# Tile 0 of the second LayerNorm transposed in four matmuls and evicted by ScalarE in three pieces, with all five engine queues in a new order

## The chip, the cores and the metric

The kernel runs on one core of one Trainium2 chip. The metric is device time in microseconds, from launch to the last output byte; lower is better. A core has five instruction queues that run side by side and wait for each other by semaphores: TensorE (PE, matmuls; its weight loads are shown as PEld), VectorE (DVE), ScalarE (ACT), GpSimd (POOL) and SyncE (SP, which here issues nearly all DMAs). Within a queue, instructions run in the order in which they stand.

## The reference

Two pre-LayerNorm blocks on a bfloat16 input of 2048 rows by 448 columns: linear attention with 16 heads of 28, then a gated MLP of width 1792.

```python
def _A_ref(x, wqkv, wo):                       # D = 448, H = 16, Dh = 28
    q, k, v = split_heads(x @ wqkv)
    phi = lambda t: jnp.where(t > 0, t + 1, jnp.exp(t)) + 1e-6
    pq, pk = phi(q), phi(k)
    kv = jnp.einsum("bhsd,bhse->bhde", pk, v)
    z = jnp.einsum("bhsd->bhd", pk)
    num = jnp.einsum("bhqd,bhde->bhqe", pq, kv)
    den = jnp.einsum("bhqd,bhd->bhq", pq, z)[..., None] + 1e-6
    return merge_heads(num / den) @ wo

def _B_ref(x, w_gate, w_up, w_down):           # width 1792
    return (gelu_tanh(x @ w_gate) * (x @ w_up)) @ w_down

h = x + _A_ref(layernorm(x), A_wqkv, A_wo)
out = h + _B_ref(layernorm(h), B_w_gate, B_w_up, B_w_down)
```

`B_x` is not used.

## The kernel before

The 2048 rows are 16 tiles of 128. The whole kernel is a list of named tasks (one queue each, one or a few instructions), built by `G.add`/`op`, which records what each reads and writes. Five strings in `ORDERS` then say, by task number, in which order each queue runs its tasks (PE, ACT, DVE, POOL, SP), and semaphore waits are derived from the recorded reads and writes. `HOLD` only picks which of several waits comes last on an instruction. A task marked `mw=True` may place a wait in front of its k-th matmul (`W(k)`) rather than its first.

Names used below (t is the tile, line numbers are those of the kernel before):

- First LayerNorm. `bnst1_t`, `bnag1_t` (DVE, L486, L487) give mean and variance, `ln1_t` and `rstd1_t` (ACT, L493, L495) the reciprocal deviation. Tiles 0 to 3: `normD_t` (DVE, L508) normalizes, `tr0_t` and `tr1_t` (PE, L516) transpose two 128-column chunks each into PSUM, `evxA_t` (ACT, L521) and `evxD_t` (DVE, L523) copy them to `xnT`. Tiles 4 to 15: `negm1_t` and `normP_t` (POOL, L490, L526) normalize, and `xT_t` (SP, L528) is a DMA transpose.
- Projections. `k_t` and `q_t` (PE, L542), four matmuls each, into one of four PSUM banks taken in turn. `ek_t`, `ck_t`, `pk_t` (ACT L553, DVE L554 and L555) make phi(k); `eq_t` and `rq_t` (ACT, L569, L570) are the exponential and the Relu of q. The first two matmuls of `k_t` read what `evxA_t` wrote, the last two what `evxD_t` wrote.
- `pt4_t`, or `pt3_t` and `pt1_t` (PE, L561), accumulate the normalized input against phi(k) over all 16 tiles. From the sums follow `z1`, `z0` (the denominator), `kv`, `kvm`, `w2_c` and their evictions `evpD_3`, `evpA_c`, `evwA_c`, `evwD_c`.
- Attention output in pairs of tiles p. Tiles 0 and 1: `t1d_0`/`t1p_1`, `dr`, `rd`, `pn` (the denominator; L598 to L604), `tro_0`, `tro_1` (PE transposes), `evo_0`, `evo_1` (ACT, L629), `out1_t` (PE, L692). Later pairs use `drP`, `rdP`, `pnP` (DVE, L614 to L617), the DMA transpose `oT_p` and `outA_p`, `outB_p` (PE, L702, L703).
- Second LayerNorm. `hr_t` (DVE, L708) adds the residual, `bnst2`, `bnag2`, `ln2`, `rstd2` as above. Tiles 0 and 1: `nhD_t` (DVE, L720) normalizes to `hn`, `wr64_t` (DVE, L722) appends a copy of columns 0 to 63 at column 448, `trh_t` (PE, L729) transposes seven 128-column chunks into PSUM, and `evhA_0` (ACT, L733) or `evhD_1` (DVE, L735) copies all seven to `hnT`. Later tiles go through POOL and the DMA transpose `hT_t`.
- Gated MLP. `gu2_v` and `gu4_v` (PE, L806 and L808) compute gate and up products side by side: the gate matmuls read partitions 0 to 63 of a chunk of `hnT`, the up matmuls partitions 64 to 127. This is why `hnT` has seven chunks for 448 columns: chunks 0 to 3 hold the columns in one arrangement, chunks 4 to 6 hold them shifted by 64, so that every 64 columns are found once in the upper and once in the lower half. `geW`, `ge0`, `ge1` (ACT, L826) are the gelu, `hm` (DVE, L828) the product, `downA_p`, `downB_p` (PE, L772) the last matmuls, `fo` and `do` the residual and the output DMA.
- `tbl2` (ACT, L837) loads the activation table of gelu. In the kernel before it stands behind everything in the list `exps`: all exponentials, all `rq_t` and `evhA_0`.

Of the kernel before, what the change touches and what calls it, by code (L numbers as in the profile page):

```python
# [8 lines left out]
AF = mybir.ActivationFunctionType  # L9
# [114 lines left out]
}  # L124


# [173 lines left out]
def bass_sequential_preLN__linear_attn_block__glu_gated_geglu__prompt_kernel(  # L300
    nc, A_x, A_wqkv, A_wo, B_x, B_w_gate, B_w_up, B_w_down, out
):
    S, D, FF, H, DH = 2048, 448, 1792, 16, 28
# [594 lines left out]
```

## Time and profile before

| | |
|---|---|
| median of 3 runs | 189.8 us (189.75 to 190.27) |
| the profiled execution | 189.66 us, of which the span of its instructions is 187.7 us |
| PE busy | 183.3 us, 98% of the span, 1822 matmuls |
| DVE, ACT, POOL busy | 129.1 us, 73.7 us, 52.6 us |

The remaining 1.96 us of the profiled execution lie outside the span. A row of the timeline view gives start, duration, engine, line, operation, tile written and tiles read, form, and in square brackets idle time ahead of it with what ended it; equal neighbours are merged and counted. A matmul row's duration includes the drain of the last one, so neighbouring rows overlap. The windows view gives the busy time of each engine in a stretch, the waits view the idle time of an engine by what ended it.

### The profile page before, as it was taken

To read this page: it belongs to the slowest core of one execution; us is meant where nothing else is said; L and a number is where in the kernel's file an instruction comes from. 1 tells how busy PE (TensorE), PEld (TensorE's weight loads), DVE (VectorE), ACT (ScalarE), POOL (GpSimd) and SP (SyncE) were. 2 spreads that over 40 slices of the span, in tenths; PEclk is the share of its full clock that TensorE was granted. 3 is DMA by queue.
4 is the path that set the end of the run, shared out by engine and by line. 5 is a ranking of instruction groups with operands and counts; after the bars stand their busy time and mean duration, and the time that the engine had idled before them with its cause. 6 is when DMAs were issued, how large, how long until landed. Compare 5 with 4: busy or idle time off the path is not lost.

```text
span 187.7 us, 4436 instructions
## 1 busy us (share of the span) xinstructions
PE 183.3 (98%) x1822; PEld 123.4 (66%) x1822; DVE 129.1 (69%) x315; ACT 73.7 (39%) x197; POOL 52.6 (28%) x91
## 2 busy tenths in 40 slices
PE   7799999999999999999999999999999999999995
PEld 7445555645699899977777777777755555454553
DVE  4999897999997999898858546362745244335432
ACT  3878752799933122324132241222242222224100
POOL 6077920524638196412460000007300000000000
PEclk9999999999999999999999999999999999999999
DMA  5994558999398316900222800000093000002024
GB/s 165 379 245 89 100 100 187 219 218 186 63 240 179 75 35 119 147 5 0 48 52 42 154 3 0 0 3 0 9 147 93 3 2 24 3 0 98 3 73 147
DMA packets 35076, 17.17 MB, mean 91 GB/s; under 512 B 26736, under 2 KB 33648, under 8 KB 35056
## 3 DMA queue, kind: packets, MB, share of 16 engines
q1 hardware_dynamic: 34432, 16.37, 40.9%
q10 hardware_dynamic: 624, 0.52, 0.8%
q8 instruction: 14, 0.23, 0.6%
q14 instruction: 6, 0.05, 0.1%
HBM read 8.26 MB, written 1.84 MB: 54 GB/s over the span
## 4 chain that ended last, share of the span: by engine, by line
PE 96%; DVE 2%; DMA 1%; issue 0%
PE ps L808 24%; PE ps L806 22%; PE ps L772 19%; PE ps L542 13%; PE ps L561 6%; PE ps L702 3%; PE ps L753 3%; PE ps L703 2%; DMA x_sb<-in_A_x_dram 1%; DVE st L486 1%; PE ps L692 1%; PE ps L729 1%; PE ps L668 0%; PE ps L516 0%; PE ps L651 0%; DVE xnn L508 0%
## 5 line engine op out<-in xcount | busy, mean ns | idle before, releaser
L808 PE MATMUL ps<-hnT,wgu_sb 64*128 64x512 bf16 (+1 forms) x490 | 88.7, 333 | 0.0
L806 PE MATMUL ps<-hnT,wgu_sb 64*128 64x512 bf16 (+1 forms) x490 | 88.5, 333 | 0.0
L826 ACT ACTIVATE gl<-ps 128x256 bf16<-128x256 f32 (+1 forms) x98 | 35.7, 415 | 88.1 <-PE ps L806 88.0
L828 DVE TENSOR_TENSOR hh<-ps,gl 128x256 bf16<-128x256 f32 (+1 forms) x98 | 41.0, 454 | 41.4 <-ACT gl L826 41.0
L808 PEld LDWEIGHTS ps<-hnT,wgu_sb 64*128 64x128 bf16 x490 | 45.4, 94 | 13.1 <-DVE hh L828 1.5
L806 PEld LDWEIGHTS ps<-hnT,wgu_sb 64*128 64x128 bf16 x490 | 45.6, 94 | 11.1 <-DVE hnT L735 0.3
L772 PE MATMUL ps<-wd_sb,hh 64*128 64x448 bf16 x392 | 40.6, 349 | 0.0
L772 PEld LDWEIGHTS ps<-wd_sb,hh 64*128 64x128 bf16 x392 | 26.6, 94 | 11.0
L542 PE MATMUL ps<-wqk_sb,xnT 128*128 128x448 bf16 x128 | 27.4, 353 | 0.0
L486 DVE BATCH_NORM_STATS2 st<-x_sb 128x6 f32<-128x448 bf16 x32 | 19.2, 610 | 1.6 <-DMA x_sb<-in_A_x_dram 1.6
L542 PEld LDWEIGHTS ps<-wqk_sb,xnT 128*128 128x128 bf16 x128 | 12.0, 98 | 11.4 <-DVE pk L555 0.7
L613 POOL TENSOR_TENSOR t<-pq,zbc 128x448 f32<-128x448 bf16 x12 | 13.1, 1113 | 17.7 <-DVE pq L611 10.7
L561 PE MATMUL ps<-pk,xnn 128*128 128x448 bf16 x64 | 13.9, 352 | 0.0
L498 POOL TENSOR_SCALAR ln<-mv 128x2 f32<-128x2 f32 x7 | 2.0, 287 | 41.3 <-DVE mv L487 41.1
L702 PE MATMUL ps<-w,pqnT 64*128 64x448 bf16 x49 | 11.5, 349 | 0.1
L703 PE MATMUL ps<-pt_sb,pqnT 64*128 64x448 bf16 x49 | 11.5, 349 | 0.0
L553 ACT ACTIVATE e<-ps 128x448 bf16<-128x448 f32 x16 | 8.6, 539 | 5.1 <-PE ps L542 5.0
L708 DVE TENSOR_TENSOR x_sb<-ps,x_sb 128x448 bf16<-128x448 f32 x16 | 9.5, 614 | 1.2 <-PE ps L703 1.2
L737 POOL TENSOR_SCALAR hn<-x_sb,nm,rs 128x448 bf16<-128x448 bf16 x14 | 10.1, 733 | 0.5
L561 PEld LDWEIGHTS ps<-pk,xnn 128*128 128x128 bf16 x64 | 6.3, 98 | 5.8 <-DVE pk L555 0.4
L555 DVE SCALAR_TENSOR_TENSOR pk<-ps,e 128x448 bf16<-128x448 f32 x16 | 9.8, 617 | 0.2
L526 POOL TENSOR_SCALAR xnn<-x_sb,nm,rs 128x448 bf16<-128x448 bf16 x12 | 9.0, 750 | 2.3 <-ACT rs L495 2.0
(80 smaller groups left out, 155.2 us busy)
## 6 DMA issues: line engine op xcount, KB each, us to landing
out_dram<-x_sb SPq DMA_DIRECT2D x15, 112.0 KB, 1.8
wd_sb<-in_B_w_down_dram SPq DMA_DIRECT2D x1, 1568.0 KB, 9.4
x_sb<-in_A_x_dram SPq DMA_DIRECT2D x3, 448.0 KB, 6.0
wgu_sb<-in_B_w_gate_dram SPq DMA_DIRECT2D x1, 896.0 KB, 11.9
wgu_sb<-in_B_w_up_dram SPq DMA_DIRECT2D x1, 896.0 KB, 16.7
wgu_sb<-in_B_w_gate_dram SPq DMA_DIRECT2D x1, 672.0 KB, 5.9
wgu_sb<-in_B_w_up_dram SPq DMA_DIRECT2D x1, 672.0 KB, 8.4
wo_sb<-in_A_wo_dram SPq DMA_DIRECT2D x1, 392.0 KB, 7.7
```

Of the source, the lines that this page charges most:

```text
L486: op("dve", lambda e: e.bn_stats(st[:, t, :], src_ap), [b_src], [b_st[t]], "bnst%s_%d" % (tag, t))
L542: ins = e.matmul(ps[:, bk, 0:D], xnT[:, t, k, :], wqk_sb[:, k, c0:c0 + D], start=(k == 0), stop=(k == 3))
L561: ins = e.matmul(ps[:, BK_PT[c], 0:D], xnn[:, t % XN_R, c * 128:(c + 1) * 128], pk[:, ip, :], start=(t == 0), stop=(t == T - 1))
L613: op("pool", lambda e, n=n: e.tensor_tensor(t1[:, n, :, 0:DH], pq[:, a + n, :].rearrange("p (h d) -> p h d", h=H), zbc[:, :].rearrange("p ...
L702: e.matmul(ps[:, BK_OUT[0], 0:D], pqnT[ra, i2, sg // 2, :], w2[ra, sg // 2, :], start=(sg == 0), stop=(sg == 5))
L703: ins = e.matmul(ps[:, BK_OUT[1], 0:D], pqnT[rb, i2, 3 + (sg + 1) // 2, :], w2s[rb, sg // 2, :], start=(sg == 0), stop=(sg == 5))
L737: op("pool", lambda e, t=t, sh=sh: e.tensor_scalar(hn[:, sh, 0:D], x_sb[:, t, :], nm2[:, t:t + 1], rs2[:, t:t + 1], ALU.add, ALU.mult), [b ...
L772: ins = e.matmul(ps[:, bko[half][n], 0:D], hh[rows, j, sl[n]], wd_sb[rows, j, :], start=(j == 0 and (half == 0 or p == 6)), stop=(j == NJ ...
L806: first = e.matmul(psG[:, jj * N:(jj + 1) * N], wgu_sb[A_, k, j * 128:(j + 1) * 128], hnT[A_, ka_, c0:c0 + N], start=(k == 0), stop=(k == ...
L808: ins = e.matmul(psU[:, jj * N:(jj + 1) * N], wgu_sb[B_, k, j * 128:(j + 1) * 128], hnT[B_, kb_, c0:c0 + N], start=(k == 0), stop=(k == NK ...
L826: G.add("act", lambda e, gi=gi, cs_=cs_, psG=psG: e.activation(gl[:, gi, cs_], psG[:, cs_], AF.Gelu_apprx_tanh), r=[b_ps[BK_G[i]]], w=b_gl ...
L828: op("dve", lambda e, dst=dst, srcU=srcU, srcL=srcL: e.tensor_tensor(dst, srcU, srcL, ALU.mult), [b_ps[BK_U[i]]] + b_glh, [b_ar[j_][t % HR ...
```

## The change

1. `trh_0` makes four transposes (chunks 0 to 3) instead of seven. `evhA_0`, one ACT instruction over seven chunks, becomes three: `evhF_0` copies chunks 0 to 3 as they are, `evhS_0` and `evhT_0` make chunks 4 to 6 by writing the upper 64 partitions of one chunk to the lower half and the other way round. `gu2_0` waits for all three.
2. `trh_0` and `trh_1` wait for `wr64` only ahead of the one transpose that needs it.
3. The list ahead of `tbl2` holds only exponentials: `rq_t` and the evictions of tile 0 are out of it.
4. `ORDERS` and `HOLD` are new for all five queues.

```diff
@@ q_tile
-            act_exp(lambda e: e.activation(pq[:, t, :], ps[:, bk, 0:D], AF.Relu), [b_ps[bk]], [b_pq[t]], "rq_%d" % t)
+            op("act", lambda e: e.activation(pq[:, t, :], ps[:, bk, 0:D], AF.Relu), [b_ps[bk]], [b_pq[t]], "rq_%d" % t, after=[tbl1])
@@ a2_pair
-                    def ftrh(e, sh=sh, tvh=tvh):
+                    def ftrh(e, W, t=t, sh=sh, tvh=tvh):
                         ins = None
-                        for k in (0, 1, 2, 4, 5, 6, 3):
+                        for m, k in enumerate((0, 1, 2, 3) if t == 0 else (0, 1, 2, 4, 5, 6, 3)):
+                            W(m)
                             ko = k * 128 if k < 4 else (k - 4) * 128 + 64
                             ins = e.transpose(tvh[:, k, :], hn[:, sh, ko:ko + 128], ident[:])
                         return ins
-                    G.add("pe", ftrh, r=[b_hn[sh], b_hnd[sh], b_ident], w=[b_ps[BK_TH[t]]], name="trh_%d" % t)
+                    G.add("pe", ftrh, r=[(b_hn[sh], 0), (b_hnd[sh], 6 if t else 3), (b_ident, 0)], w=[(b_ps[BK_TH[t]], 0)], name="trh_%d" % t, mw=True)
                     if t == 0:
-                        exps.append(op("act", lambda e, hr8=hr8, tvh=tvh: e.activation(hnT[:, :, hr8], tvh, AF.Identity), [b_ps[BK_TH[t]]], [b_hnT[t]], "evhA_%d" % t))
+                        op("act", lambda e, hr8=hr8, tvh=tvh: e.activation(hnT[:, 0:4, hr8], tvh[:, 0:4, :], AF.Identity), [b_ps[BK_TH[t]]], [b_hnT[t]], "evhF_%d" % t)
+                        op("act", lambda e, hr8=hr8, tvh=tvh: e.activation(hnT[A_, 4:7, hr8], tvh[B_, 0:3, :], AF.Identity), [b_ps[BK_TH[t]]], [b_hnS[0]], "evhS_%d" % t)
+                        op("act", lambda e, hr8=hr8, tvh=tvh: e.activation(hnT[B_, 4:7, hr8], tvh[A_, 1:4, :], AF.Identity), [b_ps[BK_TH[t]]], [b_hnS[1]], "evhT_%d" % t)
@@ gu_chunk
-                G.add("pe", fngu, r=[b_hnT[t % HR] for t in tiles] + [b_wg[j0 * 128 >= FC], (b_wu[j0 * 128 >= FC], 1)], ...
+                G.add("pe", fngu, r=[b_hnT[t % HR] for t in tiles] + (b_hnS if t0 == 0 else []) + [b_wg[j0 * 128 >= FC], (b_wu[j0 * 128 >= FC], 1)], ...
@@ ORDERS, first string (PE)
-    "30 36 38 45 47 67 54 56 72 77 63 65 80 85 71 90 76 84 105 100 89 115 120 130 104 154 119 142 134 178 166 146"
+    "30 38 36 47 45 67 56 72 54 65 63 77 80 85 71 90 76 84 105 120 100 89 115 142 104 130 119 166 191 154 134 178"
```

What the new order does is seen at three places.

PE, from `pt4_1` on, after the first four K tiles. Rows of `ps<-wqk_sb,xnT` are projections, four matmuls each; rows of `ps<-pk,xnn` are `pt4`. Before:

```order
L561 MATMUL ps<-pk,xnn 128x448 x8
L542 MATMUL ps<-wqk_sb,xnT 128x448 x8
L561 MATMUL ps<-pk,xnn 128x448 x4
L542 MATMUL ps<-wqk_sb,xnT 128x448 x12
L561 MATMUL ps<-pk,xnn 128x448 x4
```

The same place now:

```order
L562 MATMUL ps<-pk,xnn 128x448 x8
L543 MATMUL ps<-wqk_sb,xnT 128x448 x12
L562 MATMUL ps<-pk,xnn 128x448 x4
L543 MATMUL ps<-wqk_sb,xnT 128x448 x8
L562 MATMUL ps<-pk,xnn 128x448 x4
```

The row of x8 before is `q_2 k_4`, that of x12 is `k_5 q_3 k_6`; now they are `q_2 q_3 k_4` and `k_5 k_7`. Further on the K tiles run 4, 5, 7, 6, 9, 11, 8, 10, 13, 12, 14, 15 (before: 4, 5, 6, 8, 7, 10, 9, 11, 12, 13, 14, 15), and the DMA transposes `xT_t` on SP are issued as 4, 5, 7, 6, 9, 11, 8, 10, 13, 14, 12, 15 (before: 4, 5, 6, 8, 7, 10, 9, 11, 12, 13, 14, 15).

DVE, from the eviction `evxD_2` (the first COPY) on. BN_STATS are `bnst1` of tiles 4 and 5, `e1<-e1` is `ck`, SCALAR_TENSOR_TENSOR is `pk_0`, the later COPY is `evxD_3`. Before:

```order
L523 COPY xnT<-ps 128x256
L486 BN_STATS st1<-x_sb 128x6
L554 TENSOR_SCALAR e1<-e1 128x448
L487 BN_AGGR mv1<-st1 128x2
L486 BN_STATS st1<-x_sb 128x6
L555 SCALAR_TENSOR_TENSOR pk<-ps,e1 128x448
L487 BN_AGGR mv1<-st1 128x2
L523 COPY xnT<-ps 128x256
L554 TENSOR_SCALAR e1<-e1 128x448
```

Now, `normD_3` being the TENSOR_SCALAR of `xnn`, and the first row `evxD_1` and `evxD_2`:

```order
L524 COPY xnT<-ps 128x256 x2
L509 TENSOR_SCALAR xnn<-x_sb,mv1,rs1 128x448
L555 TENSOR_SCALAR e1<-e1 128x448
L487 BN_STATS st1<-x_sb 128x6
L555 TENSOR_SCALAR e1<-e1 128x448
L488 BN_AGGR mv1<-st1 128x2
L556 SCALAR_TENSOR_TENSOR pk<-ps,e1 128x448
L487 BN_STATS st1<-x_sb 128x6
L524 COPY xnT<-ps 128x256
```

`normD_3` has gone behind `evxD_2`, and `ck_1` and the statistics of tile 5 now stand between `ck_0` and `evxD_3`.

ACT, from the two `rstd2` to the second gelu. `hnT` rows are the evictions of tile 0, `pq` are `rq`, `eq` are exponentials, `gl` are gelus. Before:

```order
L495 ACTIVATE rs2<-ln2 128x1
L569 ACTIVATE eq<-ps 128x448
L495 ACTIVATE rs2<-ln2 128x1
L570 ACTIVATE pq<-ps 128x448
L569 ACTIVATE eq<-ps 128x448
L570 ACTIVATE pq<-ps 128x448
L733 ACTIVATE hnT<-ps 128x7x128
L569 ACTIVATE eq<-ps 128x448 x2
L570 ACTIVATE pq<-ps 128x448
L837 ACT_TABLE_LOAD
L826 ACTIVATE gl<-ps 128x512 x14
```

Now:

```order
L496 ACTIVATE rs2<-ln2 128x1 x2
L571 ACTIVATE pq<-ps 128x448
L570 ACTIVATE eq<-ps 128x448
L571 ACTIVATE pq<-ps 128x448
L735 ACTIVATE hnT<-ps 128x4x128
L737 ACTIVATE hnT<-ps 64x3x128
L736 ACTIVATE hnT<-ps 64x3x128
L570 ACTIVATE eq<-ps 128x448 x2
L841 ACT_TABLE_LOAD
L830 ACTIVATE gl<-ps 128x512
L571 ACTIVATE pq<-ps 128x448
L830 ACTIVATE gl<-ps 128x512
```

One Relu (`rq_13`) has moved behind the table load and the first gelu, and `rq_14` follows the second; the program holds two table loads in all, as before.

More of the change, by code (lines that the diff above doesn't have):

```diff
@@ L397, in bass_sequential_preLN__linear_attn_block__glu_gated_geglu__prompt_kernel @@
         b_hn, b_hnd, b_hnT = bufs("hn", HN_R), bufs("hnd", HN_R), bufs("hnT", HR)
+        b_hnS = bufs("hnS", 2)
         b_ar = [[_Buf("ar%d_%d" % (j, t)) for t in range(HR)] for j in range(NJ)]
@@ L809, in fngu @@
                     return ins, first
-                G.add("pe", fngu, r=[b_hnT[t % HR] for t in tiles] + [b_wg[j0 * 128 >= FC], (b_wu[j0 * 128 >= FC], 1)], w=[(b_ps[BK_G[i]], 0), (b_ps[BK_U[i]], 1)], name="gu%d_%d" % (nt, v), mw=True, half=[b_ps[BK_G[i]]])
+                G.add("pe", fngu, r=[b_hnT[t % HR] for t in tiles] + (b_hnS if t0 == 0 else []) + [b_wg[j0 * 128 >= FC], (b_wu[j0 * 128 >= FC], 1)], w=[(b_ps[BK_G[i]], 0), (b_ps[BK_U[i]], 1)], name="gu%d_%d" % (nt, v), mw=True, half=[b_ps[BK_G[i]]])
                 for hh_ in range(2 if nj == 1 else 1):
```

194 rows, old and new, of tables (HOLD, ORDERS) are left out of this document.

## The prediction

> **What bounds the kernel now.** I read the page first, then the windows view from the second transpose to the last matmul, then PE's waits.
>
> ```profile
> PE 183.3 (98%) x1822; PEld 123.4 (66%) x1822; DVE 129.1 (69%) x315; ACT 73.7 (39%) x197; POOL 52.6 (28%) x91
> PEclk9999999999999999999999999999999999999999
> 6.20:185.40 179.20, 179.12 (x1778) 119.57 (x1778) 125.22 (x304) 71.01 (x191) 49.76 (x80) 1.00 0.42 88
> ```
>
> The last row names the stretch, its length, then each engine's busy time: from 6.20 to 185.40 us PE is busy 179.12 of 179.20 us, at full granted clock. So PE's queue is the kernel. A change can shorten it only by taking PE work out or by removing short stalls that hide inside "busy" (a matmul's modelled end covers them), and it lengthens it whenever an input comes later than the matmul's turn. PE's visible waits all lie ahead of that stretch:
>
> ```profile
> PE ps L480 <- POOL eps_t L455: 1.0, 1, 1.0
> PE ps L516 <- DVE xnn L508: 1.0, 2, 0.6
> ```
>
> The first is the warm-up, the second waits for `normD_0` and `normD_1`. The DVE order up to `normD_1` is the same in both kernels, so neither moves. The hidden stalls are found by comparing equal groups, `k_0` and `q_1`, four matmuls each:
>
> ```profile
> 6.40 1.11 PE L542 MATMUL ps<-wqk_sb,xnT 128*128 128x448 bf16 x4
> 11.60 0.93 PE L542 MATMUL ps<-wqk_sb,xnT 128*128 128x448 bf16 x4
> ```
>
> `k_0` is 0.18 us too long, and its cause (`evxD_0` behind `bnst1_3`) is unchanged. All other projections keep the even pace below, 0.755 us each. So there is hardly anything to win but PE work itself, and the question is whether the new orders bring each input in time.
>
> **The change part by part.**
>
> *Transposes.* These are `trh_0` and `trh_1`, seven each, and the next PE work after them:
>
> ```profile
> 47.19 1.08 PE L729 MATMUL ps<-ident,hn 128*128 128x128 bf16 x14
> 48.20 0.36 PE L702 MATMUL ps<-w,pqnT 64*128 64x448 bf16 x1
> ```
>
> 14 of them take 48.20 - 47.19 = 1.01 us of PE's queue, 0.072 us each. Three fewer save 0.22 us, all on the path. The Trainium skill ("TensorE: Matmul & The Clock Gate", Part 4) has about 275 ns for a 128x128 transpose inside a kernel; by that figure three would save an estimated 0.83 us. The row decides.
>
> *`k_3`.* Its third matmul needs `evxD_3`, which moves back on DVE. The rows from `normD_3` to `evxD_3` before, with the PE and ACT rows they hang on (`k_1 q_0`, then `tr0_3 tr1_3`, then `k_2 k_3`; `ek_0`, `evxA_2`, `ek_1`):
>
> ```profile
> 7.57 1.68 PE L542 MATMUL ps<-wqk_sb,xnT 128*128 128x448 bf16 x8
> 9.08 0.39 PE L516 MATMUL ps<-ident,xnn 128*128 128x128 bf16 x4
> 9.31 1.70 PE L542 MATMUL ps<-wqk_sb,xnT 128*128 128x448 bf16 x8
> 7.55 0.55 ACT L553 ACTIVATE e<-ps 128x448 bf16<-128x448 f32 x1
> 7.99 0.38 ACT L521 ACTIVATE xnT<-ps 128x256 bf16<-128x256 bf16 x1
> 8.53 0.55 ACT L553 ACTIVATE e<-ps 128x448 bf16<-128x448 f32 x1 [0.16 <-PE ps L542]
> 7.59 0.40 DVE L508 TENSOR_SCALAR xnn<-x_sb,mv,rs 128x448 bf16<-128x448 bf16 x1
> 8.10 0.62 DVE L486 BATCH_NORM_STATS2 st<-x_sb 128x6 f32<-128x448 bf16 x1
> 8.63 0.26 DVE L554 TENSOR_SCALAR e<-e 128x448 bf16<-128x448 bf16 x1
> 8.81 0.18 DVE L487 BATCH_NORM_AGGREGATE mv<-st 128x2 f32<-128x6 f32 x1
> 8.90 0.60 DVE L486 BATCH_NORM_STATS2 st<-x_sb 128x6 f32<-128x448 bf16 x1
> 9.41 0.61 DVE L555 SCALAR_TENSOR_TENSOR pk<-ps,e 128x448 bf16<-128x448 f32 x1
> 9.93 0.18 DVE L487 BATCH_NORM_AGGREGATE mv<-st 128x2 f32<-128x6 f32 x1
> 10.02 0.26 DVE L523 COPY xnT<-ps 128x256 bf16<-128x256 bf16 x1
> ```
>
> Eight projection matmuls take 9.08 - 7.57 = 1.51 us, so 0.189 each. PE's totals up to `k_2` are equal, so `k_2` still starts at 9.31, `k_3` at 10.07 and its third matmul at 10.45. `k_1` now follows two transposes instead of four and ends about 0.11 earlier, so `ek_1` runs from 8.42 to 8.96. On DVE `ck_1` starts at 9.00; the spacings in the rows are then 0.18 (`ck` to `bnag`), 0.09 to 0.12 (`bnag`, 8.81 to 8.90), 0.52 (`pk`, 9.41 to 9.93) and 0.51 to 0.53 (`bnst`, 8.10 to 8.63 and 8.90 to 9.41): `bnag1_4` 9.18, `pk_0` 9.29, `bnst1_5` 9.81, `evxD_3` 10.34 to 10.60. Cross-engine release costs about 0.06 (`evxD_3`'s like, 0.03 to 0.06 between other rows), so the third matmul goes at 10.66 instead of 10.45: 0.21 us of stall, and nothing behind it can give it back, since PE was already full. `q_1` then waits for `pk_1` (start 10.34 + 0.19 + 0.09 + 0.53 = 11.15, end 11.76) and loses some 0.03. Sum 0.24; its bounds are 0 (if `ck_1` is not late) and 0.35 (if `evxA_2`, now behind `ek_1` and ending near 9.23 against `k_2`'s 9.31, is late as well).
>
> *K tiles by DMA transpose.* SP issues twelve, one at a time:
>
> ```profile
> 10.39 16.81 SPq L528 DMA_TRANSPOSE xnT<-xnn x12
> DMA to landing us min/median/max: 2.5/2.7/4.2
> ```
>
> Back to back they start about 1.30 us apart. `q_3` ahead of `k_4` gives the transposes one projection more, 0.755 us. `normP_4` is now about 0.5 later, because `ln1_4` stands behind `ek_1` and both evictions, so `xT_4` starts near 10.95. Following 1.30 a step: `xT_5` 12.3, `xT_7` 13.6, `xT_6` 14.9, `xT_9` 16.3, `xT_11` 17.6, `xT_8` 18.9, `xT_10` 20.2. Their K tiles are due on PE (before's pace, plus 0.24) at 17.1, 17.9, 19.4, 20.9, 21.65, 22.4, 23.9: 3.5 to 4.8 us after issue, above the median landing everywhere and above the largest in most. The thin one is `xT_13`: its `rstd1_13` stands on ACT behind `ek_6`, which waits for `k_6` (ends near 20.3), so `normP_13` ends at 21.8, the transpose starts at 21.83, and `k_13` is due at 24.68, 2.85 us later. At the median landing this is no stall. I cost it at 0, with the bounds 0 and 4.2 - 2.85 = 1.35.
>
> *The chain into the second LayerNorm.* `trh_0` stands right behind the last Q projection on PE:
>
> ```profile
> 33.88 0.63 DVE L598 TENSOR_TENSOR t<-pq,zbc 128x448 f32<-128x448 bf16 x1
> 45.45 1.09 DVE L614 TENSOR_REDUCE den<-t 128x32 f32<-128x928 f32 x1
> 46.45 0.39 DVE L720 TENSOR_SCALAR hn<-x_sb,mv,rs 128x448 bf16<-128x448 bf16 x1
> 47.02 0.12 DVE L722 COPY hn<-hn 128x64 bf16<-128x64 bf16 x1
> 47.46 0.18 DVE L722 COPY hn<-hn 128x64 bf16<-128x64 bf16 x1
> ```
>
> Before, `wr64_0` ended at 47.14 and `trh_0` went at 47.19, so it was already the last arrival. Now `t1d_0` is ahead of `evpD_3`, so from `t1d_0` DVE has one 128-wide eviction more to do before `drP_2`, about 0.5 us, of which some 0.1 is won at `t1d_0`'s start: `drP_2` near 45.9, `nhD_0` 46.9 to 47.25, `wr64_0` (now behind `nhD_1`) to 47.56. PE reaches `trh_0` at 47.30. The first three transposes need `nhD_0` alone and go; the fourth waits until 47.62 instead of 47.51: 0.11 us, bounds 0 and 0.3.
>
> Other short stalls of before in this stretch go: `kvm` is earlier relative to `w2_1` (about -0.09), and `trh_0`'s 0.04.
>
> *ScalarE.* The eviction before, two ACTIVATEs of 512 columns, and the table load with the gelu after it:
>
> ```profile
> 47.87 0.96 ACT L733 ACTIVATE hnT<-ps 128x896 bf16<-128x896 bf16 x1
> 41.11 1.11 ACT L629 ACTIVATE pqnT<-ps 128x512 bf16<-128x512 bf16 x2
> 50.15 1.28 ACT L837 ACT_TABLE_LOAD   x1
> 51.50 0.60 ACT L826 ACTIVATE gl<-ps 128x512 bf16<-128x512 f32 x1
> 49.77 0.38 PE L806 MATMUL ps<-hnT,wgu_sb 64*128 64x256 bf16 x2
> ```
>
> Two of 512 take 1.11, so one starts 0.5 after the other; the pieces of 384 columns lie between the 0.38 of 256 columns and the 0.55 of 448. The three pieces thus take 1.3 to 1.5 us against 0.96. With `trh_0` done near 47.8 they end near 49.2, and `gu2_0` is due at 49.74: hidden, with half a microsecond to spare. The next two exponentials bring the load to 50.1, as before; its end near 51.4 meets the end of `gu2_0` (51.45), so the table load neither gains nor costs. `rq_13` and `rq_14` run in the 0.9 us in which ACT waits between gelus: nothing.
>
> *Behind 50 us* the queues differ in single swaps (`downB_0` ahead of `gu2_8`, `outA_4` ahead of `gu2_10`, `t1p_8` ahead of `nhP_2`). Each input there comes over 0.2 us ahead of its use by the same kind of count. I cost them at 0.
>
> Sum: -0.22 + 0.24 + 0.11 - 0.09 - 0.04 = 0.00 us. The profiled execution took 189.66 us, the median of the runs is 0.14 above it, so the forecast is 189.8 us.
>
> **The rivals.**
>
> *A late transpose (slower).* If `xT_13`, or any of the ones ahead of it, lands later than its due time, PE stands still in the middle of a full queue. Landings in before spread from 2.5 to 4.2 us. For: the margin of `xT_13` is 2.85 us against a median of 2.7. Against: the largest landing belongs to one transpose alone. It decides from a landing of 2.85 us, costs up to 1.35, and at a middle landing of 3.5 gives 189.8 + 0.65 = 190.4 us. Chance 0.22, of which a bit over half beyond 190.4.
>
> *`k_3` does not stall, or the DVE chain is not late.* Then -0.22 - 0.09 - 0.04 is left: 189.4 to 189.5 us. For: 0.2 us hangs on one ACT start (`ek_1`). Against: four DVE instructions now stand between it and `evxD_3`. Chance 0.15.
>
> *Transposes cost more than their spacing (faster).* If an eviction-bound transpose occupied PE far longer than 0.072 us, removing three would give 0.7 to 0.9 us: 189.0 us. Against: the row of 14, with the next matmul behind them. The page named above stands for this price. Chance 0.03.
>
> *The forecast* keeps 0.60: 189.5 to 190.1 us.
>
> **How the numbers follow.** About 0.3% (0.57 us) is what a measurement of this kernel can tell from no change, so faster means below 189.2 and slower above 190.4. Faster: the third rival and a little of the second, 0.05. Slower: 0.14 of the first rival and 0.05 for several of the tight arrivals above missing together, 0.19. Same: 0.76. The range reaches from the second rival's lower end with the spread between runs (189.3) into the first rival, to 190.7.
>
> **What would show it.** Right: `trh_0` and `trh_1` in about 0.8 us of PE instead of 1.0; a stall of 0.2 us inside `k_3` with `evxD_3` ending near 10.6; PE's first gate matmul within 0.2 us of 49.77; the three evictions done by 49.3. Wrong: a PE gap in front of `k_13`, `k_8` or `k_6` that ends with a DMA; `gu2_0` waiting for ACT; a PE queue shorter by over 0.5 us at 49.77.

## The result and the profile after

The changed kernel takes **189.99 us** (median of 22 runs, 189.85 to 191.01) against 189.78 us for the kernel before, measured beside it (22 runs, 189.54 to 190.28): ratio 1.0022, 95% interval 1.0012 to 1.0031. The forecast of 189.8 us is 0.2 us off, and the difference it called too small to measure is there: slightly slower.

The runs fall into two groups, 14 from 189.85 to 190.09 and 8 from 190.26 to 191.01 (before: 18 up to 189.99 and 4 from 190.20 to 190.28). The first profile of the changed kernel took 190.50 us and belongs to the upper group. A second one, the run e11 below, took 189.90 us and belongs to the lower. Both are used: "the first" and "the second" profile.

The page of the first, and PE's wait in it that the kernel before does not have:

```profile
PE 184.6 (98%) x1819; PEld 131.1 (70%) x1819; DVE 128.7 (68%) x315; ACT 73.9 (39%) x199; POOL 51.3 (27%) x91
```

```profile
PE ps L543 <- DMA xnT<-xnn: 0.3, 1, 0.3
```

PE issues three matmuls fewer and is busy 1.3 us longer. That is no measure of the change: 0.9 us of it lie ahead of 6.2 us, where all 40 warm-up matmuls start 0.107 us apart (before, the last dozen 0.056), and 0.8 behind 185.4 us, because PE ends later; between the two it is busy 0.4 us less. The timeline of PE, first profile, has that wait:

```profile
14.17 1.68 PE L543 MATMUL ps<-wqk_sb,xnT 128*128 128x448 bf16 x8
16.14 0.92 PE L543 MATMUL ps<-wqk_sb,xnT 128*128 128x448 bf16 x4 [0.30 <-DMA xnT<-xnn]
```

Eight matmuls (`q_2 q_3`) take 8 x 0.189 = 1.51 us, so `k_4` was due at 15.68 and starts at 16.14: 0.46 us lost, waiting for `xT_4`. In the second profile `k_4` follows without a gap. This is most of the 0.60 us between the two profiles; 0.15 more lie at `k_0`, which keeps its stall in the first and loses hardly anything in the second.

The rest is read from the second profile. PE around `trh_0` and `trh_1` (now 11 transposes) and the first matmul of `gu2_0`:

```profile
47.27 0.78 PE L731 MATMUL ps<-ident,hn 128*128 128x128 bf16 x11
47.98 0.36 PE L703 MATMUL ps<-w,pqnT 64*128 64x448 bf16 x1
...
49.55 0.27 PE L812 MATMUL ps<-hnT,wgu_sb 64*128 64x256 bf16 x1
```

The transposes hold PE for 47.98 - 47.27 = 0.71 us instead of 1.01, and `gu2_0` starts at 49.55 instead of 49.77. At 49.6 us the changed kernel is 0.22 us **ahead**. It ends 0.24 us behind. ScalarE in that stretch:

```profile
47.69 0.60 ACT L735 ACTIVATE hnT<-ps 128x512 bf16<-128x512 bf16 x1
48.31 0.48 ACT L737 ACTIVATE hnT<-ps 64x384 bf16<-64x384 bf16 x1
48.82 0.49 ACT L736 ACTIVATE hnT<-ps 64x384 bf16<-64x384 bf16 x1
49.33 0.98 ACT L570 ACTIVATE eq<-ps 128x448 bf16<-128x448 f32 x2
50.33 1.28 ACT L841 ACT_TABLE_LOAD   x1
51.62 0.60 ACT L830 ACTIVATE gl<-ps 128x512 bf16<-128x512 f32 x1
```

The first gelu starts 0.01 us after the table load ends, with no idle time in brackets: it waited for the load, not for `gu2_0`, whose last matmul ended at 51.24. Before, load and matmuls ended almost together (51.43 and 51.47). From `evhF_0` on every row follows the one before it: ScalarE is full. VectorE then waits for that gelu, and the up matmuls of `gu2_2`, which need the PSUM bank that `hmW0_0` empties, wait for VectorE:

```profile
52.25 0.69 DVE L832 TENSOR_TENSOR hh<-ps,gl 128x512 bf16<-128x512 f32 x1 [0.38 <-ACT gl L830]
```

```profile
52.50 0.38 PE L810 MATMUL ps<-hnT,wgu_sb 64*128 64x256 bf16 x2
53.00 0.28 PE L812 MATMUL ps<-hnT,wgu_sb 64*128 64x256 bf16 x1
```

`gu2_2` takes 0.30 us longer than its equals. In the kernel before, this place had no margin either: the first up matmul of `gu2_2` (L808) already came 0.05 us behind the gate matmul beside it (L806).

```profile
52.83 0.27 PE L806 MATMUL ps<-hnT,wgu_sb 64*128 64x256 bf16 x1
52.88 0.28 PE L808 MATMUL ps<-hnT,wgu_sb 64*128 64x256 bf16 x1
```

The last loss is at 155 us, in `gu4_47`: the matmul of 155.86 was due at 155.73.

```profile
155.51 0.38 PE L812 MATMUL ps<-hnT,wgu_sb 64*128 64x512 bf16 x1
155.53 0.38 PE L810 MATMUL ps<-hnT,wgu_sb 64*128 64x512 bf16 x1
155.86 0.39 PE L812 MATMUL ps<-hnT,wgu_sb 64*128 64x512 bf16 x1
```

The 0.13 us lost there are in every profile with the new orders apart from those where VectorE has one instruction more, and in none with the old ones. So the whole sum is -0.22 + 0.30 + 0.13 = +0.21 us, and the start of `downB_6`, near the end, moves from 177.01 to 177.23, +0.22.

### The profile page after: what moved, and what is told of

It is laid out like the page before. It is cut to its first block, busy times and chain, and to the rows that moved or that the text cites. A ratio compares the mean times of both kernels' runs of the same rounds, so it can differ in the third digit from the quotient of the medians.

```text
span 188.5 us, 4429 instructions
## 1 busy us (share of the span) xinstructions
PE 184.6 (98%) x1819; PEld 131.1 (70%) x1819; DVE 128.7 (68%) x315; ACT 73.9 (39%) x199; POOL 51.3 (27%) x91
## 4 chain that ended last, share of the span: by engine, by line
PE 87%; ACT 5%; DMA 4%; DVE 2%; issue 0%
PE ps L812 33%; PE ps L776 19%; PE ps L810 11%; PE ps L543 9%; PE ps L562 5%; PE ps L757 3%; DMA xnT<-xnn 3%; PE ps L704 2%; PE ps L703 2%; DMA x_sb<-in_A_x_dram 1%; ACT eq L570 1%; ACT pq L571 1%; DVE st L487 1%; PE ps L693 1%; ACT L841 1%; ACT e L554 1%
## 5 line engine op out<-in xcount | busy, mean ns | idle before, releaser
L776 PEld LDWEIGHTS ps<-wd_sb,hh 64*128 64x128 bf16 x392 | 29.8, 94 | 8.0
L499 POOL TENSOR_SCALAR ln<-mv 128x2 f32<-128x2 f32 x7 | 1.5, 221 | 38.5 <-DVE mv L488 38.3
```

The source lines that it names most:

```text
L776: ins = e.matmul(ps[:, bko[half][n], 0:D], hh[rows, j, sl[n]], wd_sb[rows, j, :], start=(j == 0 and (half == 0 or p == 6)), stop=(j == NJ ...
```

## The experiments

All ratios are to the kernel before, measured beside each run. Late runs occur in every version, in varying number, so the lowest runs are given beside the median where the median hides an effect. "Lost" is what a group of equal matmuls takes beyond the pace of its like. "New orders" are the five queues of the changed kernel, "old orders" those of before. Diffs name tasks in their queue's order.

**Do the two parts of the change cancel?** e2 takes the new orders with the old tile 0, e3 the old orders with the new tile 0.

```diff
 e2, PE and ACT of the changed kernel:
-trh_0 (4)   evhF_0 evhT_0 evhS_0
+trh_0 (7)   evhA_0
 e3, ACT in the order of before:
-rstd2_1 rq_15 eq_14 rq_14 evhA_0               eq_12 eq_13 rq_13 tbl2 geW0_0
+rstd2_1 rq_15 eq_14 rq_14 evhF_0 evhT_0 evhS_0 eq_12 eq_13 rq_13 tbl2 geW0_0
```

> The changed kernel in its new order, but tile 0 as before: seven transposes and one eviction evhA_0. Theory (the three pieces make the gelu table late): PE does 0.27 us more in trh_0, ScalarE is done 0.8 us earlier, the table load ends before gu2_0 does and the stall of 0.29 us in gu2_2 is gone; the two cancel and the median is 189.9 to 190.05. Rival (the pieces are hidden, as predicted, and only the transposes count): 190.2 to 190.3.

> The order of the kernel before on all queues, with four transposes and the three pieces for tile 0, and nothing else. Theory: PE saves 0.27 us, ScalarE needs 0.8 us more ahead of the table load, which then ends near 52.2 instead of 51.4; gu2_2 stalls for about 0.9 us and the median is 190.3 to 190.6. Rival (pieces hidden): 189.5.

e2: 190.24 us (189.76 to 190.91, 12 runs), ratio 1.0017 (1.0000 to 1.0033). The median lies in the rival's range, but the profile (190.10) does not bear the rival out: it loses nothing at `gu2_2`, and what it loses, it loses at the start (0.35 at `k_3`, 0.21 at `k_4`). Its best runs, 189.76 to 189.81, lie below the changed kernel's 189.85, though it makes all seven transposes. These cost it 0.17 us, not the 0.27 of the expectation:

```profile
47.60 0.94 PE L731 MATMUL ps<-ident,hn 128*128 128x128 bf16 x14
48.48 0.36 PE L703 MATMUL ps<-w,pqnT 64*128 64x448 bf16 x1
```

14 transposes hold PE for 48.48 - 47.60 = 0.88 us, the changed kernel's 11 for 0.71. e3: 190.43 us (190.30 to 190.94, 11 runs), ratio 1.0029 (1.0015 to 1.0044). ScalarE of e3:

```profile
50.89 1.28 ACT L841 ACT_TABLE_LOAD   x1
52.18 0.60 ACT L830 ACTIVATE gl<-ps 128x512 bf16<-128x512 f32 x1
```

In the old order the pieces and both `rq` stand ahead of the load; it ends 0.7 us later than before, and `gu2_2` loses 0.63, `gu2_1` 0.09. `gu2_0` loses 0.21 more, waiting for VectorE's `evhD_1`. The new tile 0 alone is a loss of about 0.6 us. What moving `rq_13` and `rq_14` behind gelus is worth, e8 shows, which puts them back into the changed kernel:

```diff
-evhS_0 eq_12 eq_14 tbl2 geW0_0 rq_13 geW0_1 rq_14 geW0_2
+evhS_0 eq_12 eq_14 rq_13 rq_14 tbl2 geW0_0 geW0_1 geW0_2
```

> The changed kernel with rq_13 and rq_14 ahead of the table load, where the kernel before had them. Theory (ScalarE is full from q_10 to the first gelu, so each instruction ahead of the load delays it): the load ends 0.85 us later, gu2_2 stalls by about 1.1 us and the best runs are at 190.7. Rival (ScalarE has slack there): 189.85, unchanged.

191.11 us (190.70 to 191.79, 6 runs), ratio 1.0064 (1.0045 to 1.0083). PE loses 1.17 us (0.54 at `gu2_1`, 0.63 at `gu2_2`) where the changed kernel loses 0.30, and the best run is 190.70 against 189.85. The two Relus move the load by 0.79 us (it starts at 51.12 instead of 50.33, with the pieces done 0.08 us earlier) and cost PE 0.87: ahead of the load ScalarE has no slack at all.

**Is the late load the ScalarE time of the pieces?** e4 lets the two shifted pieces copy 8 of 128 columns of each chunk, so part of the computation is left out; a memset on POOL zeroes these chunks at the start.

```diff
-evhS_0: hnT[A_, 4:7, hr8]  <- tvh[B_, 0:3, :]       evhT_0: hnT[B_, 4:7, hr8]  <- tvh[A_, 1:4, :]
+evhS_0: hnT[A_, 4:7, 0:8]  <- tvh[B_, 0:3, 0:8]     evhT_0: hnT[B_, 4:7, 0:8]  <- tvh[A_, 1:4, 0:8]
```

> The changed kernel, in which evhS_0 and evhT_0 copy 8 of 128 columns of each chunk (the rest of these chunks of tile 0 is zero, so the products of tile 0 are not the real ones). PE's work is the same, ScalarE does some 0.6 us less ahead of the table load. Theory: the load is on time, the stall in gu2_2 goes, and the median falls by 0.25 us to about 189.7. Rival (gu2_2 waits for something else): 189.9 to 190.0, as the changed kernel.

189.80 us (189.52 to 190.81, 12 runs), ratio 1.0008 (0.9988 to 1.0027). The median does not separate it, because half of its runs lie above 190.0, but its six best lie at 189.52 to 189.56 against 189.85 to 189.90: -0.33 us. Its pieces take 0.4 us together, and the gelu now waits for PE:

```profile
50.38 1.28 ACT L842 ACT_TABLE_LOAD   x1
51.94 0.60 ACT L831 ACTIVATE gl<-ps 128x512 bf16<-128x512 f32 x1 [0.27 <-PE ps L811]
```

`gu2_2` loses nothing in this profile. So the pieces' time is what made the load late, worth 0.3 us.

**Can another engine take a piece?** e6 gives `evhT_0` to VectorE, ahead of `evhD_1`; e12 does that in the old orders.

```diff
 DVE:
 wr64_1 pnP_2
+evhT_0
 evhD_1 aqP_3
```

> The changed kernel with evhT_0 on VectorE, between pnP_2 and evhD_1, behind evhF_0. Theory: ScalarE is done 0.5 us earlier, the table load ends before gu2_0, gu2_2 loses its 0.29 us of stall; evhD_1 comes 0.35 us later and costs gu2_0 0.05 to 0.2 us. Best runs at 189.65 to 189.75. Rival (gu2_2 waits for VectorE's product and not for the table): no better than 189.85.

e6: 190.32 us (189.70 to 190.91, 12 runs), ratio 1.0019 (1.0004 to 1.0033), best runs 189.70 to 189.74, as the theory had it, but not for its reason. `gu2_0` now waits 0.22 us for `evhD_1` and `gu2_2` loses 0.09, together 0.31, no less than in the changed kernel. What was won are the 0.13 us of `gu4_47` (see e14).

e9 is the new tile 0 in the old orders with the Relus moved, and `aqP_3` behind `evhD_1`; e12 is that with the piece on VectorE.

```diff
 e9, orders of before:
 ACT: eq_12 eq_13
-     rq_13 tbl2 geW0_0 geW0_1
+     tbl2 geW0_0 rq_13 geW0_1 rq_14   (rq_14 stood ahead of tile 0's evictions)
 DVE:
-     wr64_1 aqP_3 pnP_2 evhD_1 hr_3
+     wr64_1 pnP_2 evhD_1 aqP_3 hr_3
```

> The order of the kernel before on all queues, with the four transposes, the three pieces, rq_13 and rq_14 behind the first and the second gelu, and aqP_3 behind evhD_1 (as the changed kernel has it), so that gu2_0 doesn't wait for evhD_1. Theory (the changed kernel's loss has two parts, the late table and the new start, and this has neither the new start nor Relus ahead of the table): transposes save 0.27 us, the table is still some 0.2 us late, best runs 189.4 to 189.55 against 189.53 of the kernel before. Rival (the new start gains and tile 0 loses more than that): 189.8 or above.

> As the old order with the new tile 0, with evhT_0 on VectorE ahead of evhD_1. Theory: the table load is on time, gu2_2 does not stall, and all of the 0.27 us of the transposes is left: best runs at 189.3, below the kernel before. Rival (evhD_1, 0.35 us later, holds up gu2_0): best runs at 189.45 to 189.55.

e9: 189.70 us (189.53 to 190.17, 12 runs), ratio 0.9993 (0.9980 to 1.0006); `trh_0` and `trh_1` gain 0.21 us and `gu2_2` loses 0.26; e15 below shows that VectorE holds it there, not the load alone. e12: 190.32 us (190.14 to 191.00, 12 runs), ratio 1.0030 (1.0016 to 1.0045): the load is in time, but VectorE is late with `evhD_1` (0.18 us at `gu2_0`) and with `hmW0_0` (0.57 at `gu2_2`).

**Is the quicker start of VectorE worth having?** e1 moves the one eviction that holds `k_3`; e5 puts back all of VectorE's old order up to `pk_1`; e7 is e5 and e6 together.

```diff
 e1, DVE:
 ck_1 bnag1_4 pk_0
+evxD_3
 bnst1_5
-evxD_3
 bnag1_5 bnst1_7 pk_1
 e5, DVE:
-evxD_1 evxD_2 normD_3 ck_0 bnst1_4 ck_1 bnag1_4 pk_0 bnst1_5 evxD_3 bnag1_5 bnst1_7 pk_1
+evxD_1 normD_3 evxD_2 bnst1_4 ck_0 bnag1_4 bnst1_5 pk_0 bnag1_5 evxD_3 ck_1 bnst1_7 pk_1
```

> The changed kernel with one DVE instruction moved: the eviction evxD_3 stands right behind pk_0, ahead of the statistics of tile 5. Theory (the stall in k_3 is paid in full): k_3 takes 0.97 us on PE again instead of its 1.19, and the median falls by 0.2 us against the changed kernel's 189.99, to about 189.8. Rival (the 0.22 us are given back, because a DMA transpose or ScalarE is the next one late): the stall in k_3 goes but the median stays at 189.9 to 190.0, with a longer wait in front of k_4 or in gu2_2.

> The changed kernel with VectorE's order of the kernel before from evxD_1 to pk_1 (normD_3 ahead of evxD_2, statistics of tiles 4 and 5 ahead of pk_0, ck_1 behind evxD_3), the statistics of tile 7 staying where those of tile 6 were. Theory (DVE loses about 0.3 us by waiting for the transposes of tile 2 and then for the exponential of k_1, and the loss reaches PE in k_3 or in q_1): neither k_3 nor q_1 stalls, and the best runs come down by 0.25 to 0.3 us against the changed kernel's 189.85, to about 189.6. Rival (something later limits PE, so that a quicker start is waited away): best runs stay at 189.85.

> Both edits together: VectorE's old order at the start and evhT_0 on VectorE. Theory (the two losses are apart and add up): best runs at 189.4, which is below the kernel before (its best are 189.53). Rival (they share a limit): 189.6.

e1: 190.00 us (189.94 to 190.95, 12 runs), ratio 1.0016 (0.9999 to 1.0034). `k_3` loses nothing, and `q_1` loses 0.32 instead:

```profile
9.68 0.28 DVE L524 COPY xnT<-ps 128x256 bf16<-128x256 bf16 x1
9.88 0.62 DVE L487 BATCH_NORM_STATS2 st<-x_sb 128x6 f32<-128x448 bf16 x1
...
11.14 0.60 DVE L556 SCALAR_TENSOR_TENSOR pk<-ps,e 128x448 bf16<-128x448 f32 x1
```

`evxD_3` is 0.6 us earlier, `pk_1` not at all (11.14 against 11.04), and `pk_1` frees the bank that `q_1` writes. e5: 190.25 us (190.01 to 191.05, 12 runs), ratio 1.0024 (1.0010 to 1.0038). Both of VectorE's stalls are gone, and in its profile (190.62, a late run) PE waits for transposes, 0.17 us at `k_4`, 0.31 at `k_8` and 0.34 at `k_13`. The last two stand in e4's profile as well, without this edit. Even the best run is 0.16 above the changed kernel's, so what was won is given back; where the best runs lose it is not shown. e7: 189.99 us (189.52 to 190.97, 12 runs), ratio 1.0015 (1.0000 to 1.0031): one run at 189.52 comes near the sum; the profiled one (189.93) loses it between `k_3` and `q_1` (0.29 and 0.09), at `gu2_0` (0.22) and at `gu2_2` (0.09).

**What are the two groups of runs?** e11 is the changed kernel once more, e10 puts `q_3` behind `k_4` again, e13 makes 30 warm-up matmuls instead of 40.

```diff
 e10, PE:
-q_2 q_3 k_4
+q_2 k_4 q_3
 e13:
-    WARM = 40
+    WARM = 30
```

> The changed kernel again, for a second profile of it. Theory: in a run of 189.9 us the wait of k_4 for xT_4, 0.46 us in the first profile, is absent or below 0.1 us, and the stalls in k_3 (0.22) and gu2_2 (0.29) are there. Rival: these two differ as well.

> The changed kernel with q_3 behind k_4 on PE, as before, nothing else. Theory (PE's queue runs ahead into q_3, which waits for no transpose, so its next instruction page is fetched near 13.5 us and holds up xT_4, which is then 4.4 to 5.1 us on its way): the fetch moves back to about 15 us and xT_4 lands 3.3 us after its issue, near 14.1, so that k_4 does not wait though it is due 0.75 us earlier; best runs not above 189.85, and fewer runs above 190.4. Rival (xT_4 is late for its later issue or for other transfers): it lands near 15.2 all the same, k_4 waits 0.3 to 0.5 us and the best runs are at 190.1 or above.

> The changed kernel with 30 warm-up matmuls instead of 40, so that PE's instructions reach their page borders about ten matmuls later. In the profiles of the new orders a 16 KB page of instructions is moved at 12.65 to 13.85 us and xT_4 lands 4.3 to 5.1 us after its issue; in those of the old orders the page is moved at 14.96 to 15.84 and xT_4 lands after 3.2 to 3.7. Theory (the page's transfer delays the transposes that are under way): the page moves at 14 to 15.5 us, xT_4 lands within 3.8 us of its issue, PE does not wait at k_4, and fewer than a third of the runs lie above 190.25; the fast runs stay at 189.9. Rival (it is the order of the transposes and of what loads beside them): the page moves, xT_4 still lands after 4.3 us or more, and as many runs are late as before.

e11: 189.90 us, no wait at `k_4`; its profile is the second one above. e10: 190.75 us (190.54 to 191.39, 8 runs), ratio 1.0051 (1.0033 to 1.0069). `k_4` waits 0.51 us although PE was not ahead, and the page of instructions is moved as early as in the changed kernel. That refutes the idea that PE, running ahead, calls for the page sooner. By the best runs (190.54 against 189.85) `q_3` ahead of `k_4` is worth some 0.7 us, given that `xT_4` is late; besides the wait at `k_4` the profile loses 0.38 us at `pt4_4`.

Late runs are not all of one kind. The profile of e4 (190.27, its best runs 189.54) loses nothing at `k_4` and 0.66 us at `k_8` and `k_13`:

```profile
22.62 0.93 PE L544 MATMUL ps<-wqk_sb,xnT 128*128 128x448 bf16 x4 [0.16 <-DMA xnT<-xnn]
25.24 0.93 PE L544 MATMUL ps<-wqk_sb,xnT 128*128 128x448 bf16 x4 [0.17 <-DMA xnT<-xnn]
```

There `xT_8` landed 2.5 us after its issue, but was issued at 20.09 us instead of 19.01 (second profile). In the two profiles with this delay, e4 and e5, an 8 KB page of instructions that starts at 18.5 us takes 1.25 and 1.37 us to move; pages at that time take 0.3 to 0.7 us in the others. Whether that is the cause is not shown.

e13: 191.73 us (191.44 to 192.14, 5 runs), ratio 1.0093 (1.0079 to 1.0107), which was not expected:

```profile
1.04 3.38 PE L481 MATMUL ps<-ones_bf 128*128 128x128 bf16 x30 [1.04 <-POOL ones_bf L453]
...
8.24 1.70 PE L543 MATMUL ps<-wqk_sb,xnT 128*128 128x448 bf16 x4
```

Four projection matmuls take 1.70 us instead of 0.92: they run at half speed up to `k_1`, although the profile's granted clock stands at 1.00 there. All five runs are late by 1.5 us or more. Ten warm-up matmuls less cost 1.7 us against the changed kernel's 189.99. What it was made for it shows only in part: the page moves at 17.1 us, `xT_4` lands after 2.5 us, and now the third transpose lands after 4.5. The same is seen in nineteen of the twenty profiles: the transpose issued about two to three microseconds ahead of the transfer of PE's 16 KB page of instructions is the slow one: `xT_4`, after 4.3 to 5.1 us, where the page starts at 12.65 to 13.85 (all new orders but e13); the third, after 4.0 to 4.2, where it starts at 14.96 to 15.26 (old orders). The one exception is e12, with the page at 15.84 and the third landing after 2.6. In the old orders the third has its slack, in the new ones `xT_4` has little. That the page's transfer is the cause fits this, and is not shown: e13 also changed when everything starts, and the other profiles differ in their orders too.

**Why does `gu4_47` lose 0.13 us?** e14 adds one instruction to VectorE, a memset of one column of a tile that nothing reads, at its start.

```diff
 DVE:
+nop1
 the order of the changed kernel
```

> The changed kernel with one instruction more on VectorE, at its start: a memset of a tile of one column that nothing reads, in a time in which VectorE waits. In every profile with the new orders except the two with a piece on VectorE, an 8 KB page of instructions is moved at 154 us instead of 150, hm0_44 starts 0.24 us after the gelu that it reads instead of 0.03, and PE loses 0.13 us at gu4_47. Theory (VectorE crosses the border of an instruction page at hm0_44): one instruction more moves the border to an instruction ahead of it, the page is moved near 150, hm0_44 starts 0.03 us after its gelu, PE loses nothing there, and the best runs are at 189.72 to 189.77 instead of 189.85. Rival (it is what the orders do there): hm0_44 late, 0.13 lost, best runs 189.85.

189.92 us (189.73 to 190.40, 12 runs), ratio 1.0003 (0.9993 to 1.0012). `gu4_47` loses nothing, and the best runs go from 189.85 to 189.73. VectorE of the second profile and of e14, at the first product of group 44 (their gelus start at 152.71 and 152.72):

```profile
153.33 0.76 DVE L832 TENSOR_TENSOR hh<-ps,gl 128x256 bf16<-128x256 f32 x2 [2.95 <-ACT gl L830]
```

```profile
153.14 0.76 DVE L834 TENSOR_TENSOR hh<-ps,gl 128x256 bf16<-128x256 f32 x2 [2.74 <-ACT gl L832]
```

The product that starts 0.2 us late in the changed kernel starts in time when the queue is one instruction longer, and an 8 KB page of instructions is moved at 150.0 us instead of 154.0. So this loss has nothing to do with the order there: VectorE's page border happened to fall on an instruction whose delay its queue carries on to the product that `gu4_47` waits for. The Trainium skill ("Runtime: NRT & Kernel Launch", Instruction fetch mechanics) calls the cost of crossing a border, of 16 KiB there, mostly hidden. Here, with pages of 8 KB, it is 0.2 us on VectorE, of which 0.13 reach the end.

**The piece on POOL.** POOL waits from 45.1 to 49.8 us (second profile). e15 (old orders, from e9) and e16 (new orders, with e14's instruction) let it copy `evhT_0` within `hnT`, behind `evhF_0`. e17 is e15 with `aqP_4` behind `hmW0_0`; e18 is e16 once more.

```diff
-op("act", ... hnT[B_, 4:7, hr8] <- tvh[A_, 1:4, :], "evhT_0")
+op("pool", ... tensor_copy(hnT[B_, 4:7, hr8], hnT[A_, 1:4, hr8]), "evhT_0")
 POOL: t1p_5 t1p_4
+evhT_0
 t1p_6 t1p_7 (in e15, e17 t1p_7 t1p_6)
+POOL waits: evhT_0 for t1p_4, the next t1p for evhT_0
 e17, DVE:
-bnst2_3 aqP_4 hmW0_0 drP_3
+bnst2_3 hmW0_0 aqP_4 drP_3
```

> The old orders with tile 0 in four matmuls (as in e9), evhT on POOL, which copies it within hnT behind evhF instead of reading PSUM. Theory (ScalarE is full up to the first gelu, and half a microsecond less there is worth the 0.26 us that gu2_2 lost in e9): the table load starts near 49.8, ends ahead of gu2_0's end, gu2_2 waits under 0.1, 189.45 to 189.55 us. Rival (POOL's copy comes too late): a copy over 1.2 us holds back gu2_0 and then all behind it, 189.9 or more; or the pieces of POOL that follow (t1p_6, t1p_7) are late, seen at oT_3 and outA_3.

> The changed kernel with evhT on POOL (as e15) and the extra VectorE instruction (as e14). Theory (late table load and page border are the two losses behind 45 us): gu2_2 and gu4_47 lose nothing, k_3 still 0.22: best runs 189.85 - 0.29 - 0.13 = 189.43, the late third of the runs stays. Rival (they don't add up): VectorE's evhD_1 holds back gu2_0 by 0.2 instead, as in the kernels with the piece on VectorE: 189.65.

> As e15 (old orders, tile 0 in four matmuls, evhT on POOL), with aqP_4 on VectorE moved behind hmW0_0. In e15 the table load came in time (51.01 against gu2_0's end of 51.28), but hmW0_0 started 0.35 us after its gelu, behind aqP_4 (51.40 to 52.35), and gu2_2 lost 0.255 again. Theory (hmW0_0 sets gu2_2, and VectorE's order is now what holds it): hmW0_0 starts at 51.95, gu2_2 loses nothing, 189.75 - 0.25 = 189.50 us. Rival (it moves on): aqP_4, now later, makes drP_3 and with it oT_3 and outA_3 late, or the second product hmW0_1, and the time stays at 189.7.

> e16 once more, unchanged, beside other runs of the kernel before. Theory (its gain is the two removed losses): median 189.4 to 189.55 us, ratio 0.997 to 0.999. Rival (its eight runs happened to miss the late transposes, which a third of the runs with the new orders showed): the best runs again at 189.4, but some of them 0.4 to 1.0 above, and a median of 189.6 or more.

e15: 189.75 us (189.63 to 190.54, 12 runs), ratio 0.9999 (0.9987 to 1.0011). The load is in time, and `gu2_2` still loses 0.26: VectorE comes to `hmW0_0` only at 52.27, behind `aqP_4` (0.94 us there, 0.61 before). e17: 190.04 us (189.83 to 190.88, 12 runs), ratio 1.0018 (1.0004 to 1.0031): `gu2_2` loses nothing, and `downA_0`, behind `outA_3`, loses 0.39; another 0.27 are lost at `k_3`. The rival that it moves on holds. e16: **189.45 us** (189.35 to 189.62, 8 runs), ratio 0.9979 (0.9969 to 0.9989). e18: 189.46 us (189.38 to 190.50, 12 runs), ratio 0.9989 (0.9977 to 1.0002), with five of its runs between 189.66 and 190.50. POOL and ScalarE of e16:

```profile
48.48 0.68 POOL L739 COPY hnT<-hnT 64x384 bf16<-64x384 bf16 x1 [3.26 <-ACT hnT L737]
```

```profile
48.45 0.49 ACT L738 ACTIVATE hnT<-ps 64x384 bf16<-64x384 bf16 x1
48.95 0.98 ACT L572 ACTIVATE eq<-ps 128x448 bf16<-128x448 f32 x2
49.95 1.28 ACT L843 ACT_TABLE_LOAD   x1
51.41 0.60 ACT L832 ACTIVATE gl<-ps 128x512 bf16<-128x512 f32 x1 [0.18 <-PE ps L812]
```

POOL's copy runs beside ScalarE's piece, the load ends 0.18 us ahead of need, and `gu2_2` and `gu4_47` lose nothing. The medians of the two lie 0.36 and 0.26 us below the kernel before beside them; the interval of e16 lies wholly below 1, that of e18 just includes it. It is the fastest version measured and the one to keep, with its late runs unsolved.

## Why the prediction was wrong, by its own steps

**The failed step: ScalarE "hidden, with half a microsecond to spare", "the table load neither gains nor costs".** The spare time was counted to the wrong end. The pieces are done at 49.31, 0.24 us ahead of `gu2_0`; but behind them on ScalarE stand two exponentials, the load and the first gelu, without a gap, so each tenth that the pieces take longer is a tenth by which the gelu is late. They take 49.31 - 47.69 = 1.62 us against my 1.3 to 1.5: the rows of 64 partitions begin 0.02 to 0.03 us after their forerunner ends, where two of 128 had begun 0.5 apart, overlapping by some 0.1. The load ended at 51.61 where I had "near 51.4". And it was held against `gu2_0`'s end of before, 51.45, because the sum ahead of it had come to 0.00, while the change in fact brings that end to 51.24. Both errors together are the 0.37 us by which the load is late, and 0.30 us of PE. e4 shows it by removing the time, e8 by adding to it, e16 by moving it.

**"Behind 50 us ... 0".** Wrong by 0.13 us at `gu4_47`, and beyond what the order of the queues could tell (e14).

**Transposes, -0.22, and `wr64`, +0.11.** Fewer transposes do save time on the path, but both sizes were wrong. The row of 14, divided by 14 for 0.072 us each, held a wait: `wr64_1` ended at 47.46 + 0.18 = 47.64, and `trh_1` started at 47.70, 0.11 us after its turn. Transposes that nothing holds start 0.056 us apart, so three are 0.17 us (e2). `trh_0` and `trh_1` gained 0.34 us in all; the other 0.17 are waits that are gone because only one transpose of each now waits for `wr64`: 0.11 ahead of `trh_1`, 0.04 ahead of `trh_0`, 0.02 beside them. In the old orders `trh_1` then waits as long for `nhD_1` (e3, e9); VectorE's new order, with `nhD_1` ahead of `wr64_0`, takes that away too. The prediction had a new wait of 0.11 there and 0.04 to win. The 275 ns of the Trainium skill ("TensorE: Matmul & The Clock Gate", Part 4) are the length of one transpose; a single one lasts 0.22 us here, but adds only 0.056 in a row of them, and 0.83 us for three was far off.

**`k_3`, +0.21.** Right in mechanism and size, 0.218. VectorE, second profile:

```profile
8.92 0.28 DVE L555 TENSOR_SCALAR e<-e 128x448 bf16<-128x448 bf16 x1
...
9.21 0.59 DVE L556 SCALAR_TENSOR_TENSOR pk<-ps,e 128x448 bf16<-128x448 f32 x1
9.72 0.61 DVE L487 BATCH_NORM_STATS2 st<-x_sb 128x6 f32<-128x448 bf16 x1
10.25 0.27 DVE L524 COPY xnT<-ps 128x256 bf16<-128x256 bf16 x1
```

The chain is the one worked out (`evxD_3` at 10.25, I had 10.34). What I did not see is that it cannot be had back alone: `pk_1` is next (e1), and by the profile of e5 the transposes behind it. The 0.03 for `q_1` did not come.

**`kvm`, -0.09.** It did not come: `w2_1` still loses 0.093 in both kernels.

**The rival of a late transpose.** Right as a mechanism. In the changed kernel's own profile it struck not `xT_13`, the thin one by the median landing, but `xT_4`; my list of due times began with `xT_5`. The signs named, `k_13` and `k_8`, do stall in the profiles of e4 and e5, and `k_13` in e13. In the first profile `k_4` was due at 15.68, 4.8 us after `xT_4`'s issue at 10.87, and that would have passed as well, since 4.2 was the largest landing of before. What failed is the spread: in the new orders but e13 `xT_4` lands after 4.3 to 5.1 us. Its row in the first profile:

```profile
L529 SPq DMA_TRANSPOSE xnT<-xnn x1: 1314/1314/1314, 10.9 to 10.9; - x1
...
DMA to landing us min/median/max: 5.1/5.1/5.1
```

In the first profile PE loses 0.46 us by it. That the other late runs, about a third, are of this kind is not shown.

So ahead of 49.6 us the sum was -0.22 (three transposes -0.17, waits at `trh` -0.17, `k_3` +0.21, -0.07 at `k_0`, which the first profile does not have, and -0.02 not assigned), where I had 0.00; behind it +0.43, where I had 0.00. That 189.8 us came within 0.2 us is luck: a gain of 0.22 us that was not counted hid half of a loss that was not counted. What stays open is why the page of PE's instructions is moved one to two and a half microseconds earlier in the new orders, and whether it is that which makes `xT_4` late.

## What to carry to other kernels

When an operation on a side engine grows, count not to its own consumer but along its queue to the next thing that the busy engine needs; where rows there follow each other without idle time, "hidden" is not to be had. Hold an arrival against the due time of the changed kernel, not of before: work saved on the bottleneck makes everything else due earlier by as much. And where a gain is given back, look for the idle engine at that very place (here POOL) before tuning the order of the full ones.

## What the runs showed of the hardware

- ACTIVATEs that read one half of the partitions and write the other (64x384) did not overlap their neighbours: each starts 0.02 to 0.03 us after the previous end (second profile, e3, e9), where rows of 128 partitions overlap by about 0.1. The Trainium skill ("ScalarE: Activation LUTs", What ACT_TABLE_LOAD costs) has consecutive ACTIVATEs overlap by about 93 ns; these do not.
- An instruction of VectorE started 0.2 us late, and an 8 KB instruction page was moved right behind it; with one more instruction 150 us earlier the page was moved 4 us sooner and the instruction was in time (e14).
- Transposes of 128x128 start 0.056 us apart in a row (14 in 0.88 us in e2, 11 in 0.71 in the second profile, change-over to the next matmuls included).
- Thirty warm-up matmuls in 3.4 us instead of forty in 4.3 left the next projections at half speed (0.37 us each instead of 0.19) up to `k_1`, with a granted clock that read 1.00, and cost 1.7 us (e13). Full speed came at 3.9 us in the profile before, between 5.6 and 6.2 us in the second and at 10.2 us in e13. The Trainium skill ("TensorE: Matmul & The Clock Gate", Part 1) puts the warm-up at about 3.4 us of sustained work in a window that runs freely, which leaves 30 matmuls at the edge. The traces agree in that the moment is not fixed, but the page has it vary by 0.5 us, and here it moves by several.
- In nineteen of twenty profiles the DMA transpose issued about two to three microseconds ahead of the transfer of PE's 16 KB instruction page near 13 to 17 us landed after 4.0 to 5.1 us; the quickest transposes land after 2.4.
